# An attention pass with its steps in another order, 64x64 mask matmuls, and one block of cleared rows

## The chip, the core and the metric

The program runs on one core of a Trainium2 chip. Its engines run side by side, each through its own queue in order: TensorE (PE; PEld are its weight loads), VectorE (DVE), ScalarE (ACT), GpSimd (POOL) and SyncE (SP, which here only issues transfers). They wait for each other through semaphores. The metric is the device time of one execution in microseconds; lower is better.

## The reference

Attention for 8 x 8 heads of 576 positions and 64 dimensions, in two parts that are added: one over q, k and v averaged over four positions (144 positions, a full softmax), one over a local band. Then a layer of 8 experts for the 4608 rows of 512: each row goes to the one expert with the largest gate.

```
out_d = sm_attn(q_d, k_d, v_d)                  # mean over 4 positions
out_up = np.repeat(out_d, factor, axis=2)
mask = np.abs(pos[:, None] - pos[None, :]) < factor
scores = np.where(mask, scale * np.matmul(q, k.transpose(0, 1, 3, 2)), -1000000000.0)
out_local = np.matmul(softmax(scores), v)
x = (out_up + out_local) as rows of tokens
y[token] = gate[token] * (np.maximum(x @ w1[e], 0.0) @ w2[e])   # e = the token's expert
```

## The kernel before, in words

**Passes.** The attention runs in 32 passes, one for each pair of heads. The table `PASS` (L768) is the order of the steps inside a pass, written by hand. An entry `(step, lag)` does that step for pair `i - lag` while pass `i` runs, so up to five pairs are in work at once (lag -1 works ahead). As every engine takes its instructions in program order, this table alone sets the order on each engine. After the last pass three drain passes run, and then the stage of the experts.

Steps for the local band of pair i: `s_loc` (TensorE; mask matmuls L229, then 40 score matmuls L235, into pS, of which there is one), `max_loc` (VectorE L248), `sub_loc` (L252), `exp_loc` (ScalarE L255), `sums` (VectorE L258), `eps` (ScalarE L261), `inv` (VectorE L266, the reciprocal), `norm` (L270), `t_loc` (TensorE transposes L308 in two parts), `e_loc` (ScalarE copies them, L315), `pv_loc` (L336). For the averaged part: `pool_qk`, `pool_qk2`, `pool_v`, `pool_v2` on GpSimd; `s_d` (TensorE L284, into pD, of which there is one), `max_d` (L289), `max_scale` (L292), `exp_d` (ScalarE L298), `norm_d` (VectorE L273), `t_d` (L321), `e_d` (L329), `pv_d` (L349), `out_d` (ScalarE L353). `add_up` (VectorE L363) joins the two. The reciprocal of pair i-1 is written into the bank pD of pair i, so `inv` stands behind `s_d` of the running pass; `s_d` in turn waits for `exp_d` of the pass before, which reads the one pD. In the built program `exp_d` also waits for `norm_d` of the same pass.

**The router.** Entries that begin with "@" are slots for work on finished rows: `@ra` (40 or 32 router matmuls L381), `@rb` (their transposes L392 and L394, VectorE L397 to L408, an exponential L401), `@rc` (ranks and places: VectorE L423 to L436, ScalarE L426 and L428), `@x` (transposes L443 to rows, copied at L445), `@sc` (scatters of 128 rows to the table `xs`, a memset and an indirect transfer on GpSimd, L467 and L468), and `@w1` (a quarter of expert weights split on ScalarE L180 and GpSimd L181, passes 15 to 30). a, b and c of one group of rows fall into passes i, i+1 and i+2, a new group every four passes from pass 6; scatters run from pass 9. Transposes and router share three banks called pX.

**Loads.** At the start of pass i SyncE is given qk(i+2), vd(i+1) and vw(i), and in a few passes 512 KB of expert weights (raw). Three buffers each for qk and vw, two for vd, decide when a load can go.

**Cleared rows.** The table `xs` has for each expert a region with room; the rows behind the last token must read as padding. Its first 128 rows belong to no expert. At pass 20 SyncE writes the padding block `pad` (128 rows of 514, in SBUF) to them (L815) and to a table of its own, `zs` (L816). In the stage of the experts `pad_after` (L458) copies from `zs` behind an expert's rows. A write to `xs` is ordered behind the scatters that are out.

Of the kernel before, what the change touches and what calls it, by code (L numbers as in the profile page):

```python
# [90 lines left out]
def attention_moe_kernel(ctx: ExitStack, tc: tile.TileContext, qk, vw, vd, wg, w1, w2, cst, csb, out):  # L91
# [18 lines left out]
        return psX.tile([128, 512], F32, name="pX", bufs=3)  # L110

    xs = dram.tile([ROW0 + E * CAP, ROW], F32, name="xs")
    zs = dram.tile([128, ROW], F32, name="zs")

    QK, VW, VD, QKD, VDS, A, AD, AT, XT, MXD, SMD, ADT, PS_, PD, PV, IV, QKT, VDT, MX, BX = ({} for _ in range(20))

# [107 lines left out]
    def s_loc(i):  # L224
        p = psS.tile([128, 1024], F32, name="pS")
        PS_[i] = p
        for s in range(2):
            r = slice(s * 64, s * 64 + 64)
            nc.tensor.matmul(p[:, s * 512:s * 512 + NC * KW], selb[r], maskb[r], start=True, stop=False,  # L229
                             tile_position=(s * 64, 0), skip_group_check=True)  # L230
        x = QK[i]
        for c in range(NC):
            for h, t in ((0, 0), (1, 1), (0, 1), (1, 0)):
                g, s, r = NC * t + c, h ^ t, slice(h * 64, h * 64 + 64)
                nc.tensor.matmul(p[t * 64:t * 64 + QB, s * 512 + c * KW:s * 512 + (c + 1) * KW],  # L235
                                 x[r, g * QB:(g + 1) * QB],
                                 x[r, QPAD + g * QB:QPAD + g * QB + KW],
                                 start=False, stop=(c == NC - 1), skip_group_check=True)
# [219 lines left out]
    def pad_after(e):  # L458
        rs = nc.s_assert_within(rows_end(e), ROW0 + e * CAP, ROW0 + e * CAP + N, skip_runtime_bounds_check_because=why)
        nc.sync.dma_start(xs[bass.ds(rs, BASE), DM:].rearrange("(t p) c -> p t c", p=128),  # L460
                          zs[:, None, DM:].to_broadcast([128, BASE // 128, ROW - DM]))
        nc.sync.dma_start(xs[bass.ds(rs, 256), :DM].rearrange("(t p) c -> p t c", p=128),
                          zs[:, None, :DM].to_broadcast([128, 2, DM]))

    def scatter(m, t):
        xr = xrs[:, x_slot(m, t)]
# [297 lines left out]
    def at(k, fn, *a):  # L764
        todo.setdefault(k, []).append(lambda: fn(*a))


    PASS = (  # L768
        (s_loc, 0), (max_loc, 0), (pv_loc, 3), (pv_d, 3), (out_d, 3), (t_d, 2, 0), (e_d, 2, 0), (t_loc, 2, 1),
        (pool_qk, -1), (sums, 1), (s_d, 0), (eps, 1), (sub_loc, 0), (add_up, 3), (inv, 1), ("@rb",),  # L770
        (e_loc, 2, 1), (t_d, 2, 1), (t_loc, 2, 0), ("@sc",), (exp_loc, 0), (pool_qk2, -1), (max_d, 0),
        (e_d, 2, 1), (norm, 1), (e_loc, 2, 0), ("@rc",), (norm_d, 1), (pool_v, 0), ("@w1",), (max_scale, 0),
        ("@x",), (exp_d, 0), (pool_v2, 0), ("@ra",),
    )

    def steps(i):
# [29 lines left out]
    for i in range(NP):  # L806
        for fn, have, want in ((load_qk, QK, i + 2), (load_vd, VD, i + 1), (load_vw, VW, i)):
            for j in range(len(have), min(want, NP - 1) + 1):
                fn(j)
        if i == 2:  # L810
            nc.gpsimd.tensor_copy(crun, cf[:, C_CAP:C_CAP + E])
        if i in PADS:
            pad_first(PADS.index(i))
        if i == 20:
            nc.sync.dma_start(xs[0:ROW0, :], pad)  # L815
            nc.sync.dma_start(zs, pad)  # L816
        steps(i)
        if i + 1 < len(WARM):
            warm(WARM[i + 1], i >= 3)
        if i in RAW:  # L820
            raw_ahead(RAW.index(i) + 1)
        if i == NP - 1:
            close_p1.close()
            close_s.close()
            _, mp[0] = pool(name="m1", bufs=1)
            _, mp["p1"] = pool(name="psM1", bufs=2, space=PSUM)
            x_load(0, 0)
            gi_load(0, 0, 2)
            raw_ahead(8)
# [136 lines left out]
```

## Time and profile before

| what | us |
|---|---|
| median of three runs (656.22 to 662.75) | 657.36 |
| the profiled execution's own time | 659.0 |
| its span, first to last instruction | 657.2 |
| start of the maximum of pass 8, 20, 21, 24, 31 | 45.63, 118.09, 123.97, 145.47, 187.23 |

The span is what the trace shows; the time of an execution lies a little around it. A pass is read here from one start of VectorE's maximum (L248) to the next. In the rows, an idle time in brackets stands before the instruction, with what ended it ("issue": nothing that the profile shows).

### The profile page before, as it was taken

Reading aid. Unit: us, or ns where it says so; the run is one execution under the profiler, and the core shown is the slowest. Engines: PE = TensorE matmul, PEld = TensorE weight load, DVE = VectorE, ACT = ScalarE, POOL = GpSimd, SP = SyncE. Lnnn points to the kernel's source line nnn. Section 1 sums busy time; section 2 is a strip of 40 time slices with the busy share of each in tenths; the row PEclk is TensorE's granted clock in tenths of the full one; section 3 lists DMA queues with packets and bytes.
Section 4 is the critical chain, followed back from the end, with each engine's and each line's share of the span. In section 5 each row is a group of like instructions: output and inputs, shape, how many; then the busy total and the mean of one; then the engine's idle time right before and its main releaser. Section 6 shows DMA issues by size and latency. Waiting matters only on the chain.

```text
span 657.2 us, 15596 instructions
## 1 busy us (share of the span) xinstructions
PE 624.1 (95%) x6160; PEld 508.1 (77%) x6163; DVE 363.3 (55%) x674; ACT 321.3 (49%) x845; POOL 224.2 (34%) x333
## 2 busy tenths in 40 slices
PE   7999999899998989999999999999999999999994
PEld 4777777677777888888888888888888778888873
DVE  6999988878984565481481174175138047115020
ACT  3777777868874544452452263264235145224120
POOL 7968778798872410111111101111010101110111
PEclk9999999989998999999999999999999989999998
DMA  8999887987753496274284258248137528110001
GB/s 289 298 238 298 258 291 234 280 278 252 261 151 130 151 299 193 89 178 146 75 215 146 65 151 219 66 136 210 64 112 178 180 76 220 38 46 1 33 18 41
DMA packets 66226, 108.52 MB, mean 165 GB/s; under 512 B 15388, under 2 KB 36524, under 8 KB 66112
## 3 DMA queue, kind: packets, MB, share of 16 engines
q1 hardware_dynamic: 59984, 87.89, 46.8%
q0 software_dynamic: 5984, 19.01, 7.8%
q8 instruction: 66, 1.08, 0.7%
q14 instruction: 48, 0.39, 0.2%
q10 hardware_dynamic: 144, 0.15, 0.1%
HBM read 86.98 MB, written 23.67 MB: 168 GB/s over the span
## 4 chain that ended last, share of the span: by engine, by line
PE 72%; issue 10%; DVE 7%; DMA 3%; POOL 3%; ACT 3%; POOLq 0%; another core or an unknown queue 0%; SPq 0%; ACTq 0%; DVEq 0%
PE p L592 8%; PE p L593 8%; PE p L594 8%; PE p L606 7%; PE p L608 7%; PE p L607 7%; PE pD L284 3%; PE pS L235 2%; PE pX L308 2%; PE pX L321 2%; PE pX L443 2%; PE pX L688 2%; PE pX L707 2%; PE pPV L349 2%; PE pPV L336 1%
## 5 line engine op out<-in xcount | busy, mean ns | idle before, releaser
L592 PE MATMUL p<-xh,w1h 128*128 128x512 f32 (+1 forms) x288 | 107.3, 372 | 3.8 <-issue 1.8
L613 POOL DMA_INDIRECT out_dram<-y,tix x39 | 37.9, 973 | 210.4 <-ACT y L625 199.0
L593 PE MATMUL p<-xl,w1h 128*128 128x512 f32 (+1 forms) x288 | 106.4, 369 | 0.7 <-DVE xl L540 0.7
L594 PE MATMUL p<-xh,w1l 128*128 128x512 f32 (+1 forms) x288 | 106.2, 369 | 0.0
L606 PE MATMUL p<-w2h,hh 128*128 128x512 f32 x256 | 101.1, 395 | 0.0
L608 PE MATMUL p<-w2h,hl 128*128 128x512 f32 x256 | 99.8, 390 | 0.0
L607 PE MATMUL p<-w2l,hh 128*128 128x512 f32 x256 | 99.8, 390 | 0.0
L597 DVE SCALAR_TENSOR_TENSOR hl<-p,hh 128x512 fp32r<-128x512 f32 (+1 forms) x72 | 45.5, 632 | 96.6 <-ACT hh L596 96.4
L596 ACT ACTIVATE hh<-p 128x512 fp32r<-128x512 f32 (+1 forms) x72 | 39.8, 553 | 81.9 <-PE p L594 80.4
L625 ACT ACTIVATE y<-p,gi 128x512 f32<-128x512 f32 x32 | 22.1, 691 | 92.6 <-PE p L608 88.2
L592 PEld LDWEIGHTS p<-xh,w1h 128*128 128x128 f32 x288 | 55.1, 191 | 13.8 <-issue 2.2
L593 PEld LDWEIGHTS p<-xl,w1h 128*128 128x128 f32 x288 | 55.2, 192 | 9.8 <-DVE xl L540 0.9
L594 PEld LDWEIGHTS p<-xh,w1l 128*128 128x128 f32 x288 | 55.1, 191 | 9.0
L608 PEld LDWEIGHTS p<-w2h,hl 128*128 128x128 f32 x256 | 48.0, 188 | 10.3
L607 PEld LDWEIGHTS p<-w2l,hh 128*128 128x128 f32 x256 | 48.1, 188 | 10.1 <-DVE w2l L582 0.6
L606 PEld LDWEIGHTS p<-w2h,hh 128*128 128x128 f32 x256 | 48.1, 188 | 9.4
L468 POOL DMA_INDIRECT xs<-xr,ix x36 | 36.0, 1001 | 24.6 <-ACT re L401 10.9
L540 DVE TENSOR_TENSOR xl<-pX,xh 128x512 fp32r<-128x512 f32 x38 | 24.7, 684 | 35.2 <-ACT xh L539 34.2
L582 DVE TENSOR_TENSOR w2l<-raw,w2h 128x512 fp32r<-128x512 f32 x64 | 43.5, 682 | 0.8 <-ACT w2h L581 0.6
L298 ACT ACTIVATE AD<-pD,mxd 128x144 f32<-128x144 f32 x96 | 35.6, 380 | 13.6 <-DVE AD L273 10.9
L180 ACT ACTIVATE w1h<-raw 128x512 fp32r<-128x512 f32 (+1 forms) x72 | 41.6, 578 | 0.0
L215 POOL TENSOR_TENSOR vdt<-vd 72x512 f32<-72x512 f32 x32 | 40.8, 1275 | 0.1
(149 smaller groups left out, 1220.3 us busy)
## 6 DMA issues: line engine op xcount, KB each, us to landing
raw<-in_w_dram SPq DMA_DIRECT2D x64, 512.0 KB
qk<-in_qk_dram SPq DMA_DIRECT2D x32, 583.0 KB
vw<-in_vw_dram SPq DMA_DIRECT2D x32, 320.0 KB
vd<-in_vd_dram SPq DMA_DIRECT2D x32, 288.0 KB
xrow<-xs SPq DMA_DIRECT2D x32, 192.0 KB
xrow<-xs SPq DMA_DIRECT2D x32, 128.0 KB
xs<-zs SPq DMA_DIRECT2D x6, 512.0 KB
xs<-pad SPq DMA_DIRECT2D x3, 257.0 KB
```

The lines of the kernel that those rows point to most:

```text
L180: nc.scalar.activation(hi[:, s], src[:, s], AF.Copy)
L215: nc.gpsimd.tensor_add(t2, v[:, 0:2], v[:, 2:4])
L582: nc.vector.tensor_sub(lo, src, hi)
L592: nc.tensor.matmul(p, wh[:, fs], xh[:, k, r], start=(k == 0), stop=False)
L593: nc.tensor.matmul(p, wh[:, fs], xl[:, k, r], start=False, stop=False)
L594: nc.tensor.matmul(p, wl[:, fs], xh[:, k, r], start=False, stop=(k == 3))
L596: nc.scalar.activation(hh[:, f, r], p, AF.Relu)
L597: nc.vector.scalar_tensor_tensor(hl[:, f, r], p, 0.0, hh[:, f, r], op0=OP.max, op1=OP.subtract)
L606: nc.tensor.matmul(p, hh, wh, start=(f == 0), stop=False)
L607: nc.tensor.matmul(p, hh, wl, start=False, stop=False)
L608: nc.tensor.matmul(p, hl, wh, start=False, stop=(f == 7))
L613: ins = nc.gpsimd.indirect_dma_start(out=out, out_offset=bass.IndirectOffsetOnAxis(ap=ix, axis=0), in_=y, in_offset=None, bounds_check=N - ...
```

## The change

The order in `PASS` is another one (lags and slots are the same). The mask is added by four matmuls on 64x64 tiles in place of two on 64x128. `zs` is gone: `pad_after` copies from the first 128 rows of `xs`, and these are written in pass 8.

```diff
--- before.py
+++ after.py
@@ -110,7 +110,6 @@
         return psX.tile([128, 512], F32, name="pX", bufs=3)
 
     xs = dram.tile([ROW0 + E * CAP, ROW], F32, name="xs")
-    zs = dram.tile([128, ROW], F32, name="zs")
 
     QK, VW, VD, QKD, VDS, A, AD, AT, XT, MXD, SMD, ADT, PS_, PD, PV, IV, QKT, VDT, MX, BX = ({} for _ in range(20))
 
@@ -224,13 +223,14 @@
     def s_loc(i):
         p = psS.tile([128, 1024], F32, name="pS")
         PS_[i] = p
-        for s in range(2):
-            r = slice(s * 64, s * 64 + 64)
-            nc.tensor.matmul(p[:, s * 512:s * 512 + NC * KW], selb[r], maskb[r], start=True, stop=False,
-                             tile_position=(s * 64, 0), skip_group_check=True)
+        quads = ((0, 0), (1, 1), (0, 1), (1, 0))
+        for h, t in quads:
+            s, r, o = h ^ t, slice(h * 64, h * 64 + 64), slice(t * 64, t * 64 + 64)
+            nc.tensor.matmul(p[o, s * 512:s * 512 + NC * KW], selb[r, o], maskb[r], start=True, stop=False,
+                             skip_group_check=True)
         x = QK[i]
         for c in range(NC):
-            for h, t in ((0, 0), (1, 1), (0, 1), (1, 0)):
+            for h, t in quads:
                 g, s, r = NC * t + c, h ^ t, slice(h * 64, h * 64 + 64)
                 nc.tensor.matmul(p[t * 64:t * 64 + QB, s * 512 + c * KW:s * 512 + (c + 1) * KW],
                                  x[r, g * QB:(g + 1) * QB],
@@ -458,9 +458,9 @@
     def pad_after(e):
         rs = nc.s_assert_within(rows_end(e), ROW0 + e * CAP, ROW0 + e * CAP + N, skip_runtime_bounds_check_because=why)
         nc.sync.dma_start(xs[bass.ds(rs, BASE), DM:].rearrange("(t p) c -> p t c", p=128),
-                          zs[:, None, DM:].to_broadcast([128, BASE // 128, ROW - DM]))
+                          xs[0:ROW0, None, DM:].to_broadcast([128, BASE // 128, ROW - DM]))
         nc.sync.dma_start(xs[bass.ds(rs, 256), :DM].rearrange("(t p) c -> p t c", p=128),
-                          zs[:, None, :DM].to_broadcast([128, 2, DM]))
+                          xs[0:ROW0, None, :DM].to_broadcast([128, 2, DM]))
 
     def scatter(m, t):
         xr = xrs[:, x_slot(m, t)]
@@ -766,11 +766,11 @@
 
 
     PASS = (
-        (s_loc, 0), (max_loc, 0), (pv_loc, 3), (pv_d, 3), (out_d, 3), (t_d, 2, 0), (e_d, 2, 0), (t_loc, 2, 1),
-        (pool_qk, -1), (sums, 1), (s_d, 0), (eps, 1), (sub_loc, 0), (add_up, 3), (inv, 1), ("@rb",),
-        (e_loc, 2, 1), (t_d, 2, 1), (t_loc, 2, 0), ("@sc",), (exp_loc, 0), (pool_qk2, -1), (max_d, 0),
-        (e_d, 2, 1), (norm, 1), (e_loc, 2, 0), ("@rc",), (norm_d, 1), (pool_v, 0), ("@w1",), (max_scale, 0),
-        ("@x",), (exp_d, 0), (pool_v2, 0), ("@ra",),
+        (s_loc, 0), (sums, 1), (pool_qk, -1), (max_loc, 0), (pv_loc, 3), ("@rb",), (pv_d, 3), (t_loc, 2, 1),
+        (sub_loc, 0), (out_d, 3), (t_loc, 2, 0), (e_loc, 2, 1), (e_loc, 2, 0), (pool_qk2, -1), (t_d, 2, 0),
+        ("@sc",), (s_d, 0), (eps, 1), (e_d, 2, 0), (add_up, 3), (exp_loc, 0), (inv, 1), (pool_v, 0), ("@w1",),
+        (pool_v2, 0), (t_d, 2, 1), (max_d, 0), (norm, 1), ("@ra",), (e_d, 2, 1), ("@x",), (max_scale, 0),
+        (norm_d, 1), ("@rc",), (exp_d, 0),
     )
 
     def steps(i):
@@ -811,9 +811,8 @@
             nc.gpsimd.tensor_copy(crun, cf[:, C_CAP:C_CAP + E])
         if i in PADS:
             pad_first(PADS.index(i))
-        if i == 20:
+        if i == 8:
             nc.sync.dma_start(xs[0:ROW0, :], pad)
-            nc.sync.dma_start(zs, pad)
         steps(i)
         if i + 1 < len(WARM):
             warm(WARM[i + 1], i >= 3)
```

The changed file has one line less ahead of L113, so its line numbers there are smaller by one up to s_loc and after it again; names tell which is which.

VectorE in pass 27, in which the router's steps b fall (mx is the maximum, smd the sums, pD the reciprocal, rm to oh the router, A<-pS the subtraction, XT add_up). Before:

```order
L248 TENSOR_REDUCE mx<-pS 128x10
L258 TENSOR_REDUCE smd<-A 128x10
L252 TENSOR_TENSOR A<-pS,mx 128x2x5x64
L363 TENSOR_TENSOR XT<-pPV,outd_117 128x580
L266 RECIPROCAL pD<-smd 128x13
L397 TENSOR_REDUCE rm<-pX 128x5
L399 TENSOR_TENSOR pX<-pX,rm 128x40
L403 SCALAR_TENSOR_TENSOR pX<-pX,cf 128x40
L406 TENSOR_REDUCE rm<-pX 128x5
L408 TENSOR_TENSOR oh<-pX,rm 128x40
L289 TENSOR_REDUCE mxd<-pD 128x3
```

The same place in the changed kernel:

```order
L258 TENSOR_REDUCE smd<-A 128x10
L248 TENSOR_REDUCE mx<-pS 128x10
L397 TENSOR_REDUCE rm<-pX 128x5
L399 TENSOR_TENSOR pX<-pX,rm 128x40
L403 SCALAR_TENSOR_TENSOR pX<-pX,cf 128x40
L406 TENSOR_REDUCE rm<-pX 128x5
L408 TENSOR_TENSOR oh<-pX,rm 128x40
L252 TENSOR_TENSOR A<-pS,mx 128x2x5x64
L363 TENSOR_TENSOR XT<-pPV,outd_116 128x580
L266 RECIPROCAL pD<-smd 128x13
L289 TENSOR_REDUCE mxd<-pD 128x3
```

The sums now stand ahead of the maximum, and the router's five steps ahead of the subtraction and the reciprocal.

TensorE in the same pass, from the scores to the rows of tokens (pX<-cf,AD are t_d, pX<-cf,A t_loc, pD s_d, pX<-cf,lg the router's transposes). Before:

```order
L235 MATMUL pS<-qk 58x64 x20
L336 MATMUL pPV<-AT,vw 64x58 x20
L349 MATMUL pPV<-ADT,vds 64x144 x4
L321 MATMUL pX<-cf,AD 72x112 x3
L308 MATMUL pX<-cf,A 128x128 x2
L284 MATMUL pD<-qkd 64x144 x6
L392 MATMUL pX<-cf,lg 128x128
L394 MATMUL pX<-cf,lg 128x32
L321 MATMUL pX<-cf,AD 72x112 x3
L308 MATMUL pX<-cf,A 128x128 x3
L443 MATMUL pX<-cf,XT 128x128 x4
```

And in the changed kernel:

```order
L235 MATMUL pS<-qk 58x64 x20
L336 MATMUL pPV<-AT,vw 64x58 x20
L392 MATMUL pX<-cf,lg 128x128
L394 MATMUL pX<-cf,lg 128x32
L349 MATMUL pPV<-ADT,vds 64x144 x4
L308 MATMUL pX<-cf,A 128x128 x5
L321 MATMUL pX<-cf,AD 72x112 x3
L284 MATMUL pD<-qkd 64x144 x6
L321 MATMUL pX<-cf,AD 72x112 x3
L443 MATMUL pX<-cf,XT 128x128 x4
```

All five transposes of A stand ahead of s_d, and the router's transposes ahead of pv_d. (The list counts an fp32 matmul once; the trace shows two records for each.)

SyncE around pass 20, before:

```order
L119 DMA qk<-in_qk_dram 128x1166
L192 DMA vd<-in_vd_dram 72x1024
L196 DMA vw<-in_vw_dram 128x640
L815 DMA xs<-pad 128x514
L816 DMA zs<-pad 128x514
L119 DMA qk<-in_qk_dram 128x1166
```

And around pass 8 in the changed kernel:

```order
L118 DMA qk<-in_qk_dram 128x1166
L191 DMA vd<-in_vd_dram 72x1024
L195 DMA vw<-in_vw_dram 128x640
L815 DMA xs<-pad 128x514
L118 DMA qk<-in_qk_dram 128x1166
```

One write stands between the loads of pass 8 and pass 9 in place of two between those of pass 20 and 21.

## Rows read from the trace of the kernel before

**Rows 1.** Busy time by stretch; columns as the first line of the view names them.

```profile
core 0: us, PE busy (x) PEld busy (x) DVE busy (x) ACT busy (x) POOL busy (x), PEclk, DMA share, GB/s
45.63:123.97 78.34, 73.32 (x1708) 58.13 (x1705) 70.15 (x148) 60.12 (x216) 61.94 (x80) 1.00 0.86 270
123.97:145.47 21.50, 18.22 (x366) 14.16 (x367) 15.92 (x30) 14.51 (x52) 18.52 (x26) 0.92 0.93 285
145.47:187.23 41.76, 39.56 (x928) 31.73 (x923) 37.18 (x76) 34.85 (x126) 37.18 (x49) 1.00 0.73 238
45.63:69.15 23.52, 22.09 (x531) 17.60 (x530) 21.40 (x44) 17.82 (x64) 18.20 (x24) 1.00 0.91 291
...
151.30:175.35 24.05, 22.38 (x520) 17.82 (x522) 21.50 (x46) 19.13 (x69) 21.62 (x29) 1.00 0.77 252
```

**Rows 2.** VectorE in order of time: start, us, instruction, idle before and releaser.

```profile
62.73 0.82 DVE L248 TENSOR_REDUCE mx<-pS 128x10 f32<-128x640 f32 x1 [0.94 <-PE pS L235]
...
86.53 0.82 DVE L248 TENSOR_REDUCE mx<-pS 128x10 f32<-128x640 f32 x1 [1.15 <-PE pS L235]
...
105.57 0.82 DVE L248 TENSOR_REDUCE mx<-pS 128x10 f32<-128x640 f32 x1 [0.53 <-PE pS L235]
...
111.72 0.82 DVE L248 TENSOR_REDUCE mx<-pS 128x10 f32<-128x640 f32 x1 [1.16 <-PE pS L235]
...
156.82 0.82 DVE L248 TENSOR_REDUCE mx<-pS 128x10 f32<-128x640 f32 x1 [0.55 <-PE pS L235]
...
162.97 0.83 DVE L248 TENSOR_REDUCE mx<-pS 128x10 f32<-128x640 f32 x1 [1.16 <-PE pS L235]
...
180.87 0.82 DVE L248 TENSOR_REDUCE mx<-pS 128x10 f32<-128x640 f32 x1 [0.47 <-PE pS L235]
...
187.23 0.82 DVE L248 TENSOR_REDUCE mx<-pS 128x10 f32<-128x640 f32 x1 [1.38 <-PE pS L235]
```

**Rows 3.** VectorE in order of time, pass 26: after the sums, and the last step.

```profile
157.56 0.81 DVE L258 TENSOR_REDUCE smd<-A 128x10 f32<-128x640 f32 x1
158.29 0.81 DVE L252 TENSOR_TENSOR A<-pS,mx 128x640 f32<-128x640 f32 x1
...
161.21 0.60 DVE L273 TENSOR_TENSOR AD<-AD,pD 128x432 f32<-128x432 f32 x1
```

**Rows 4.** TensorE in order of time, end of pass 26 and start of pass 27.

```profile
159.78 0.49 PE L308 MATMUL pX<-cf,A 128*128 128x128 f32 x3
...
160.64 1.30 PE L381 MATMUL pX<-XT,wgt 128*32 128x128 f32 x40
161.87 0.31 PE L229 MATMUL pS<-cb 64*128 64x320 bf16 x2
162.11 0.79 PE L235 MATMUL pS<-qk 64*58 64x64 f32 x40
162.72 0.75 PE L336 MATMUL pPV<-AT,vw 64*64 64x58 f32 x40
```

**Rows 5.** SyncE and TensorE in order of time, passes 20 and 22.

```profile
118.67 0.33 SPq L196 DMA_DIRECT2D vw<-in_vw_dram  x1
121.76 0.34 SPq L815 DMA_DIRECT2D xs<-pad  x1
...
122.62 0.45 SPq L119 DMA_DIRECT2D qk<-in_qk_dram  x1
...
129.62 0.33 PE L235 MATMUL pS<-qk 64*58 64x64 f32 x8 [1.16 <-issue]
```

**Rows 6.** The page: its head and a row of its transfer issues.

```profile
span 657.2 us, 15596 instructions
...
zs<-pad SPq DMA_DIRECT2D x1, 257.0 KB
```

**Rows 7.** VectorE's waits, passes 8 to 31 (us, times, longest); TensorE in pass 27.

```profile
DVE pX L403 <- ACT re L401: 1.6, 5, 0.3
...
167.27 0.55 PE L308 MATMUL pX<-cf,A 128*128 128x128 f32 x3 [0.93 <-ACT re L401]
```

**Rows 8.** ScalarE in order of time, start of pass 27.

```profile
161.91 0.38 ACT L298 ACTIVATE AD<-pD,mxd 128x144 f32<-128x144 f32 x1 [0.24 <-DVE AD L273]
```

**Rows 9.** GpSimd's waits from 85.4 to 193.4 us (us, times, longest).

```profile
POOL w1l L181 <- ACT w1h L180: 9.3, 6, 2.7
```

## The prediction

> **What bounds the kernel now.** The stages first: the table of busy time by stretch [rows 1]. From the maximum of pass 8 (45.63 us) to that of pass 31 (187.23 us) lie 23 passes in 141.6 us. VectorE is busy there for 70.15 + 15.92 + 37.18 = 123.25 us, so 18.35 us are idle; TensorE is busy 131.1 us, GpSimd 117.6. Nothing has much room, but VectorE is the engine whose idle time can be read: its matter is to be late once per pass. The reader is to see three unlike stretches: 78.34 us for 13 passes (6.03 each), 21.50 us for only three (7.17 each), 41.76 us for seven (5.97). After the passes comes the stage of the experts, TensorE's own matmuls one behind the other; the change doesn't touch its order, so what the passes give back should reach the end.
>
> Then VectorE's own rows. Its maximum (L248) has to wait for the scores: eight waits outside the long stretch, 0.94, 1.15, 0.53, 1.16, 0.55, 1.16, 0.47 and 1.38 us [rows 2], 7.34 us in all. Between them nothing is idle: in pass 26 the sums start 0.74 us after the maximum, and the last multiplication ends at 161.81, 4.99 us after it [rows 2, 3].
>
> Why the scores are late is in TensorE's rows [rows 4]. Behind the second part of the transposes (L308) stand the tokens' rows and, one pass in four, the 40 router matmuls: 1.23 us from their start to the masks. Masks and scores follow, and VectorE's maximum begins 0.25 us after the next step (162.72) has begun on TensorE. So a pass with the router makes TensorE some 1.2 us longer than VectorE, and VectorE has nothing else in its queue ahead of the maximum. In the pass after, the router's VectorE steps make VectorE the longer one: work and waiting lie in the wrong passes.
>
> Last the long stretch. SyncE issues vw at 118.67 (0.33 us) and then stands until 121.76, when the write of cleared rows (L815) may go: it writes the table that the scatters write, and waits for the last of them. The next qk load leaves at 122.62 [rows 5]. The held loads and two writes of 257 KB [rows 6] leave together; in the stretch behind it the DMA share is 0.93, the highest shown in [rows 1]. In the middle of 40 score matmuls, where no semaphore is waited for, TensorE stands for 1.16 us (it resumes at 129.62) [rows 5], and the granted clock of the stretch is 0.92 against 1.00 before and behind it [rows 1]: part of it ran at the lower level, 1.2 GHz.
>
> **The change, part by part.**
> *The cleared rows.* In pass 8 no scatter is out yet (the first is in pass 9), so L815 has nothing to wait for and the loads behind it aren't held; the second block (zs), 257 KB, is gone, and the later pads read the rows of xs instead: same bytes, off TensorE's path. Three passes at the mean of the other twenty, (78.34 + 41.76) / 20 = 6.01 us, are 18.0; the stretch took 21.50: **-3.5 us**. Ends: 0 if the wait only coincided with the slow passes, -3.5 if it is the cause; I take the latter, because hole, clock and DMA share stand together right behind it. Against it: pass 8 gets 257 KB; at the 291 GB/s of passes 8 to 11 [rows 1] that is 0.9 us of transfers in front of loads that are needed about two passes later: I take a third, **+0.3**.
>
> *The sums first.* VectorE now does the sums of the pass before (0.73 us from start to start, 157.56 to 158.29 [rows 3]) ahead of the maximum. Their input was made a pass earlier, so they run while the scores are late. Each wait falls by the smaller of itself and 0.73: 0.73, 0.73, 0.53, 0.73, 0.55, 0.73, 0.47, 0.73, together **-5.2 us**. This holds only if nothing waits instead. Next in line is the reciprocal: it waits for the downsampled scores (L284), and TensorE now reaches them one group of transposes later, since all five L308 stand ahead of them; the 0.49 us recorded for the three moved ones [rows 4] would come back in any pass where TensorE is the late one. What covers it is the second move: the router's VectorE steps, which stood behind the reciprocal, now stand ahead of the subtraction, in just the pass that follows the long TensorE pass. Ends: 0 (all comes back at the reciprocal) to -16.7 (all idle time, less the 1.6 us in which the router's steps wait for ScalarE within themselves [rows 7]).
>
> *The router on the other engines.* Its transposes go ahead of pv_d on TensorE; before, the three L308 waited 0.93 us for a bank that ScalarE's exponential held back [rows 7], and ScalarE stood too. Now that exponential is ahead of the copies, and the banks are needed later. I count no gain: it is the same lateness that the first term already prices. Steps c go behind norm_d on VectorE and ahead of exp_d on ScalarE, two small instructions; exp_d starts as soon as norm_d is through (161.91 [rows 8]) and VectorE has steps c to do meanwhile: 0.
>
> *GpSimd.* pool_qk2 goes ahead of the scatters, so each scatter and its memset leave one such step later and the second halving a scatter earlier; the rows are read only after the passes: 0. The w1 piece goes ahead of steps c on ScalarE; GpSimd stood 9.3 us for it in six waits [rows 9]. That is room on an engine off the path, no term of its own. On SyncE only the write moves; qk, vd and vw keep their order.
>
> *The masks.* Four matmuls of 64x64 for two of 64x128, with 64 more weight loads and matmuls in all. Now 0.24 us pass from the first mask to the first score matmul [rows 4]. The nearest rows are those behind them: 40 score matmuls in the same four tiles and the same order go in 0.61 us, 15 ns each [rows 4], which they can only do side by side. So four masks should take what two took: 0. Ends per pass: -0.1 (part of the 0.24 is the change of tile) to +0.72 (four in a row at 0.24 each).
> The Trainium skill, "TensorEngine Tiling (Array Packing)", section Restrictions and Gotchas, speaks against it: matmuls of different row tiles can't use one PSUM bank at the same time. The first two masks have different row tiles and one bank. The scores have the same pairs, and their rows don't bear the rule out.
>
> **Sum.** 659.0 (the profiled execution; its span is 657.2 [rows 6]) - 3.5 + 0.3 - 5.2 = 650.6 us. The median of the three runs, 657.36, lies 1.64 us below the profiled one: **649.0 us**.
>
> **Rivals.**
> *The transfers or GpSimd take over.* At the forecast a pass takes 6.0 - 0.35 = 5.65 us, four of them 22.6. In passes 8 to 11 the DMA engines work 0.91 of 23.52 us = 21.4, so their share would be 0.95; GpSimd has 21.62 us of work in 24.05 where it also splits w1 [rows 1]. For it: both leave about 1 us in four passes. Against: VectorE waits for no load in these rows, and passes 8 to 11 ran at 0.91 without one. Then only the long stretch gives: 659.0 - 3.2 - 1.6 = 654.2. Chance 0.25.
> *More comes back.* The router's lateness goes with the sums' and VectorE runs near its floor: half of the way from 5.2 to 16.7, some 6 us more, 643. Chance 0.10. Against it: holes like that of [rows 5] have no cause in the order and stay.
> *The masks don't overlap*, the slower side. Place: between the last transposes and the scores, each pass. TensorE is busy 22.38 of 24.05 us [rows 1], 0.42 us free per pass; below that an addition mostly hides, above it TensorE sets the pass. One after the other: +0.72, of which 0.30 x 23 passes = 6.9 us show, and nothing of the sums' gain is left: 659.0 + 6.9 - 1.6 = 664.3, or 661.1 with the 3.2 us of the long stretch. Chance 0.06. In pairs, +0.24 a pass: at most 5.5 us, 654.5; chance 0.04. By the Trainium skill's rule on banks, named above, it would be the pairs.
>
> **Numbers.** Forecast, 649.0 with a range of its own of 646 to 652: 0.55. A measurement of this kernel tells about 1% (6.6 us) from no change, so faster means below 650.8: four fifths of the forecast, the 0.10 with more, a little of the rest: 0.58. Within 1%: the other fifth, nearly all of the first rival, the pairs: 0.36. Slower: 0.06. The range that leaves out 2 in 10 reaches from the better case, 643, over the first rival to 656.
>
> **What would show it.** Right: the maximum's waits for the scores sum to under 3 us between passes 8 and 31, with the sums in the row ahead; the reciprocal waits for L284 less than 1 us in all; SyncE's L815 follows vw without a gap; the three passes behind pass 20 take about 18 us at a granted clock of 1.00; four masks and then the first score after 0.24 us; the maximum of pass 31 near 179. Wrong: idle time ahead of the reciprocal that grows as that of the maximum falls; GpSimd or loads named as releasers of VectorE or TensorE; a hole in the scores at another pass with the clock at its lower level; score matmuls that start 0.4 us or more behind the masks; or passes that shrink and an expert stage that begins no earlier.

## The result, and the profile after

The changed kernel took 652.81 us (median of four runs, 651.46 to 663.92) against 656.79 us of before (four runs too): 0.9881 of it, with an interval of 0.9833 to 0.9929. Its profiled execution took 653.26 us, with a span of 651.5. Measured twice more, with 12 runs each time, it came out at 0.9974 (0.9934 to 1.0014) and 0.9969 (0.9933 to 1.0005): some 2 us, and both intervals still hold "no change". The forecast of 649.0 promised 8.4 us. The ratios leave disturbed runs out, so they differ a little from those of the medians.

Busy time by stage: from max_loc of pass 8 to that of pass 31, from there to the first L606, and from there to the end (columns as in [rows 1]). First the changed kernel, then a second profile of before:

```profile
46.15:186.12 139.97, 129.57 (x2990) 106.08 (x2992) 127.77 (x253) 105.85 (x386) 120.11 (x156) 0.98 0.84 262
186.12:221.13 35.01, 29.77 (x425) 25.93 (x417) 21.21 (x54) 20.71 (x63) 13.94 (x29) 1.00 0.45 139
221.13:651.48 430.35, 419.62 (x1923) 347.73 (x1921) 180.94 (x300) 163.36 (x298) 54.69 (x106) 0.99 0.44 125
```

```profile
45.74:181.97 136.23, 128.52 (x2987) 102.32 (x2984) 123.36 (x253) 108.62 (x393) 117.15 (x154) 1.00 0.89 274
181.97:216.59 34.62, 30.93 (x425) 27.16 (x417) 21.89 (x56) 20.36 (x59) 15.66 (x31) 0.95 0.43 141
216.59:652.85 436.26, 421.49 (x1923) 348.90 (x1921) 180.66 (x299) 163.39 (x297) 54.87 (x106) 0.99 0.45 123
```

The reader is to see three things. The passes of before took 136.2 us this time, not 141.6 as in [rows 1]: one kernel's passes differ by more than 5 us between two executions. VectorE's busy time doesn't: 123.25 and 123.36 us before, 127.77 after. And the experts, whose order nothing touched, are 5.9 us shorter here.

VectorE's waits in the passes of the changed kernel (us, times, longest):

```profile
DVE pD L266 <- PE pD L284: 3.5, 2, 2.1
DVE rm L397 <- PE pX L394: 1.6, 1, 1.6
DVE pX L403 <- ACT re L401: 1.0, 3, 0.3
DVE pD L266 <- PE pX L443: 0.8, 1, 0.8
DVE pD L266 <- ACT A L255: 0.8, 1, 0.8
```

The waits of max_loc for the scores are gone, but for one of 0.3 us (9.1 us in eight in the second profile of before). In their place stand waits ahead of the reciprocal and the router's maximum (the latter behind a hole of TensorE of 1.3 us in pass 27).

TensorE and SyncE in order of time: the masks of pass 28, and the cleared rows of pass 8.

```profile
166.56 0.33 PE L229 MATMUL pS<-cb 64*64 64x320 bf16 x4
166.72 0.73 PE L235 MATMUL pS<-qk 64*58 64x64 f32 x40
```

```profile
45.58 0.34 SPq L195 DMA_DIRECT2D vw<-in_vw_dram  x1
45.97 0.82 SPq L815 DMA_DIRECT2D xs<-pad  x1
46.84 0.42 SPq L118 DMA_DIRECT2D qk<-in_qk_dram  x1
```

Four masks need 0.16 us up to the first score, two needed 0.24 [rows 4]; the median of the passes is the same. The four start within 0.01 us of each other. SyncE doesn't stand any more.

Where the busy time of VectorE grew: steps c of pass 24, and GpSimd at the same time.

```profile
147.95 0.17 DVE L425 TENSOR_REDUCE gt<-re 128x4 f32<-128x32 f32 x1
148.05 0.18 DVE L430 TENSOR_TENSOR rk<-pX,oh 128x32 f32<-128x32 f32 x1
148.14 0.89 DVE L431 TENSOR_TENSOR crun<-crun,cs 128x8 f32<-128x8 f32 x1
148.95 0.17 DVE L433 TENSOR_REDUCE pos<-rk 128x4 f32<-128x32 f32 x1
149.16 0.61 DVE L435 CAST ix<-pos 128x4 int32<-128x4 f32 x1
149.69 0.17 DVE L436 RECIPROCAL xr<-gt 128x4 f32<-128x4 f32 x1
```

```profile
147.85 1.16 POOL L203 TENSOR_TENSOR qkt<-qk 128x576 f32<-128x576 f32 x1
149.08 0.67 POOL L209 TENSOR_TENSOR qkd<-qkt 128x288 f32<-128x288 f32 x1
```

An addition of 8 elements takes 0.89 us and ends as GpSimd's halving ends; the cast behind it ends with the next halving. In the first profile of before the same two took 0.16 and 0.17 us, and GpSimd was standing for w1l at that time (1.50 us, up to 150.88).

```profile
150.17 0.16 DVE L431 TENSOR_TENSOR crun<-crun,cs 128x8 f32<-128x8 f32 x1
150.51 0.17 DVE L435 CAST ix<-pos 128x4 int32<-128x4 f32 x1
150.88 0.73 POOL L181 TENSOR_TENSOR w1l<-raw,w1h 128x256 fp32r<-128x256 f32 x1 [1.50 <-ACT w1h L180]
```

The second profile of before shows that the order alone is not the reason: in its pass 24 GpSimd did not stand, and there, in the old order, the two took 0.79 and 0.56 us.

### The profile page after: what moved, and what is told of

Read it like the earlier page. It is cut to its first block, busy times and chain, and to the rows that moved or that the text cites. A ratio compares the mean times of both kernels' runs of the same rounds, so it can differ in the third digit from the quotient of the medians.

```text
span 651.5 us, 15716 instructions
## 1 busy us (share of the span) xinstructions
PE 619.4 (95%) x6224; PEld 509.2 (78%) x6227; DVE 368.7 (57%) x674; ACT 318.4 (49%) x845; POOL 225.1 (35%) x333
## 4 chain that ended last, share of the span: by engine, by line
PE 70%; issue 11%; DVE 9%; POOL 3%; DMA 3%; ACT 3%; POOLq 0%; another core or an unknown queue 0%; SPq 0%; DVEq 0%; ACTq 0%
PE p L593 8%; PE p L592 8%; PE p L594 8%; PE p L606 7%; PE p L608 7%; PE p L607 7%; PE pD L284 3%; PE pX L321 2%; PE pX L688 2%; PE pX L707 2%; PE pS L235 2%; PE pPV L336 1%; PE pPV L349 1%; PE pX L308 1%; DVE A L270 1%
## 5 line engine op out<-in xcount | busy, mean ns | idle before, releaser
L592 PE MATMUL p<-xh,w1h 128*128 128x512 f32 (+1 forms) x288 | 105.9, 368 | 1.1 <-DVE hl L597 0.8
L606 PE MATMUL p<-w2h,hh 128*128 128x512 f32 x256 | 101.2, 395 | 0.0
L606 PEld LDWEIGHTS p<-w2h,hh 128*128 128x128 f32 x256 | 48.1, 188 | 9.4
```

The lines of the kernel that those rows point to most:

```text
L592: nc.tensor.matmul(p, wh[:, fs], xh[:, k, r], start=(k == 0), stop=False)
L606: nc.tensor.matmul(p, hh, wh, start=(f == 0), stop=False)
```

## The experiments

All in one table: passes (max_loc of pass 8 to 31), middle, experts (first L606 to the end) of each profile in us, the median of the runs, and the ratio to before on the same chip with its interval. Before had a median of 660.33 beside changed again, order alone, counts in PSUM and max first, 657.28 beside masks alone, rows alone, code shift and sums alone, and 657.25 beside the last four. Order alone and code shift have 6 runs, max first 11, the others behind the first comparison 12.

```
kernel                  passes  middle  experts  median  ratio
before, first profile   141.60  35.07   434.88
changed, first profile  139.97  35.01   430.35   652.81  0.9881 (0.9833-0.9929)
changed again           140.73  35.66   431.13   657.39  0.9974 (0.9934-1.0014)
order alone             136.31  34.23   436.88   655.38  0.9871 (0.9814-0.9928)
counts in PSUM          135.92  34.91   430.89   654.02  0.9881 (0.9843-0.9919)
max first               141.61  34.43   430.05   654.95  0.9923 (0.9889-0.9957)
masks alone             139.85  35.26   430.56   657.70  1.0024 (0.9996-1.0052)
rows alone              134.19  37.03   437.16   657.52  1.0022 (0.9985-1.0059)
code shift              146.96  36.73   434.51   668.86  1.0213 (1.0161-1.0264)
sums alone              135.46  35.37   436.88   657.78  1.0009 (0.9973-1.0046)
before again            136.23  34.62   436.26   656.05  0.9994 (0.9961-1.0027)
counts again            134.60  36.17   430.86   652.19  0.9938 (0.9902-0.9974)
order and counts        134.89  36.06   433.45   654.40  0.9955 (0.9917-0.9993)
changed, third          137.22  37.61   430.19   654.71  0.9969 (0.9933-1.0005)
```

**The size of the gain**: the changed kernel again (no edit).

> The changed kernel once more, unaltered, for the size of the gain. In the pair of profiles the attention passes end only 1.1 us earlier (max_loc of pass 31 at 186.12 us against 187.23), while the stage of the experts is 4.1 us shorter (427.2 us against 431.3); of these 4.1, the profile of before has one TensorE hole of 1.8 us and a stretch at half clock at 528 us, and another half-clock stretch at 200 us. Theory A: those are accidents of one execution, the gain of the medians is 3 to 4.5 us (ratio 0.993 to 0.995), and a new profile shows the experts at any length between 427 and 431 us. Theory B: the new order makes the experts themselves shorter; then the stage is 427 us again and the ratio is near 0.991.

The gain is smaller than theory A had it, but the experts took 431.1 us again (the 427 us of the expectation count from a later start), as theory B had it. That called for the next three.

**The order alone.**

```diff
-        (s_loc, 0), (max_loc, 0), (pv_loc, 3), (pv_d, 3), (out_d, 3), (t_d, 2, 0), (e_d, 2, 0), (t_loc, 2, 1),
...
+        (s_loc, 0), (sums, 1), (pool_qk, -1), (max_loc, 0), (pv_loc, 3), ("@rb",), (pv_d, 3), (t_loc, 2, 1),
...
```

> Before with the new order of steps alone: two mask matmuls of 128 rows, the cleared rows and their second block at pass 20 as before. Theory A: the order carries the whole gain; the masks and the cleared rows are worth under 0.5 us each, so the time equals that of the changed kernel within 1 us, and max_loc waits for the scores hardly at all (under 1 us between passes 8 and 31, against 10.9). Theory B (the term on record for the cleared rows): the stand of SyncE at pass 20 costs 3.5 us, so this kernel is 3 to 4 us slower than the changed one. Whichever holds, the steps of the router behind norm_d should take 1.9 us in place of 0.95, since the order of GpSimd is the same as in the changed kernel.

```profile
46.55:182.86 136.31, 129.19 (x2947) 103.33 (x2945) 128.60 (x254) 105.81 (x386) 119.60 (x155) 1.00 0.88 271
```

max_loc's waits for the scores, here and then in the second profile of before:

```profile
DVE mx L248 <- PE pS L235: 1.7, 2, 1.3
```

```profile
DVE mx L248 <- PE pS L235: 9.1, 8, 1.6
```

Beside the second profile of before, with the same masks and rows, this is the cleanest pair. max_loc waits 7.4 us less, and VectorE's idle time falls from 136.23 - 123.36 = 12.87 us to 136.31 - 128.60 = 7.71: 2.2 us of other idle time have come. Its busy time grows by 5.24, and the passes are as long as they were. The time of six runs is nevertheless below that of before, and below the changed kernel's on that chip. I read nothing from it: the first four runs of the changed kernel gave a ratio as low, and longer series did not bear it out. The 3 to 4 us of theory B aren't there, and theory A's match within 1 us isn't either. The additions and casts (busy us and mean ns between the bars), here and in the second profile of before:

```profile
L431 DVE TENSOR_TENSOR crun<-crun,cs 128x8 f32<-128x8 f32 x6 | 3.5, 583 | 0.0
L435 DVE CAST ix<-pos 128x4 int32<-128x4 f32 (+1 forms) x6 | 3.1, 524 | 0.2
```

```profile
L431 DVE TENSOR_TENSOR crun<-crun,cs 128x8 f32<-128x8 f32 x6 | 1.6, 267 | 0.0
L435 DVE CAST ix<-pos 128x4 int32<-128x4 f32 (+1 forms) x6 | 1.4, 236 | 0.2
```

That is (583 - 267 + 524 - 236) ns x 6 = 3.6 of the 5.24 us. Most of the rest lies with sub_loc, which in the passes without the router's steps b now stands right behind max_loc and waits for its result. In the changed kernel:

```profile
143.54 0.81 DVE L248 TENSOR_REDUCE mx<-pS 128x10 f32<-128x640 f32 x1
144.39 0.82 DVE L252 TENSOR_TENSOR A<-pS,mx 128x640 f32<-128x640 f32 x1
```

It starts 0.85 us behind it, where independent steps start 0.74 us apart [rows 2, 3]. In five of the 23 passes the router's steps stand between the two, so it is 0.11 us in 18 passes: 2.0 us, 0.6 of them idle and the others busy.

**The two small tiles in PSUM.**

```diff
-        cs = rp.tile([128, E], F32, name="cs")
+        cs = p[:, 64:64 + E]
-        pos = rp.tile([128, 5], F32, name="pos")
+        pos = p[:, 80:85]
```

> The changed kernel with two small tiles of the router (the count cs and the position pos) put into the PSUM bank that the step already holds; no instruction is moved. In the changed kernel the addition of the counts takes 515 ns on average (160 before) and the cast of the positions 316 to 466 ns (172 before); each ends where a GpSimd instruction ends (148.95 us and 149.69 us in pass 25). Theory A: a VectorE operation that has all its operands in SBUF stands until GpSimd's running operation on SBUF is done. With one operand in PSUM it does not; then the addition is back near 0.2 us and the cast near 0.2 us in all passes, VectorE is 3.4 us less busy over the passes, and the time falls by 2 to 3.5 us (to 0.995 to 0.997 of the changed kernel). Theory B: the two operations wait for something that belongs to their place behind norm_d (a tensor that is late, the row of instructions); then they stay at 0.4 to 0.5 us and the time does not move. Theory C: they get short, but the passes are held by loads or TensorE, and the time does not move.

The addition and the cast are back at 0.15 and 0.16 us, as theory A has it. Run a second time:

> The changed kernel with cs and pos in PSUM, once more, unaltered, beside the changed kernel on the same chip. Theory A (VectorE stands at GpSimd's operations only where all operands lie in SBUF): 2 to 5 us faster than the changed kernel again (the first time the means were 652.4 and 657.0 us), additions of the counts and casts under 0.2 us. Rival: the first difference was the luck of that chip; then the two are within 1.5 us.

Steps c of the second run's pass 24, and GpSimd at the same time:

```profile
145.13 0.15 DVE L431 TENSOR_TENSOR crun<-crun,pX 128x8 f32<-128x8 f32 x1
145.32 0.20 DVE L433 TENSOR_REDUCE pX<-rk 128x4 f32<-128x32 f32 x1
145.55 0.16 DVE L435 CAST ix<-pX 128x4 int32<-128x4 f32 x1
```

```profile
144.80 1.14 POOL L203 TENSOR_TENSOR qkt<-qk 128x576 f32<-128x576 f32 x1
```

The same halving runs, and neither operation waits for it. VectorE's busy time in the passes is 125.32 and 125.04 us, against 127.77, 128.86 and 128.70 in the changed kernel's three profiles. The medians lie 3.4 us (654.02 for 657.39) and 2.5 us (652.19 for 654.71) below the changed kernel's on the same chips, and both ratios to before are below 1 with their intervals: on both chips the fastest version of those run eleven times or more. The Trainium skill, "SBUF — State Buffer", section "SBUF: two separate sides", says that VectorE and GpSimd share a pair of ports, that one instruction holds it to its end, and that a VectorE operation with two inputs in SBUF meets there a GpSimd operation that reads SBUF, as does one in a two-port mode. The rows agree for the addition (two inputs in SBUF). The cast has one, so by that rule it must run in such a mode, which no row shows. The reductions beside them have one input in SBUF and don't wait (0.17 us for L425 at 147.95 us, during the same halving). As L425 goes from SBUF to SBUF, theory A's wording, "all its operands in SBUF", is too wide.

**max_loc first again.**

```diff
-        (s_loc, 0), (sums, 1), (pool_qk, -1), (max_loc, 0), ...
+        (s_loc, 0), (pool_qk, -1), (max_loc, 0), (sums, 1), ...
```

> The changed kernel with the sums of the pass before behind max_loc again, between it and sub_loc; all else as in the changed kernel. Theory A (the term on record: the sums cover the end of the scores): max_loc waits for the scores again, some 8 to 11 us over the passes, while each pass wins back 0.11 us because an independent step stands again between max_loc and sub_loc (23 passes, 2.5 us); in sum 3 to 6 us slower than the changed kernel. Theory B: in the new order the scores are early anyway, because t_d and e_d that stood ahead of them were moved; then the waits stay under 2 us and the kernel is 1 to 2.5 us faster than the changed one.

max_loc's waits come back, 6.0 us in seven:

```profile
DVE mx L248 <- PE pS L235: 6.0, 7, 1.3
```

Yet the kernel isn't slower than the changed one (0.9923 against 0.9974, the intervals overlap). So theory A is right in that waits come back, if fewer than its 8 to 11 us, and its price of 3 to 6 us is out; theory B has the waits wrong, and whether its gain is there stays open. In this order no gain from the place of the sums can be seen: what they cover, the dependent pair behind them and other waits may well cost.

**The sums alone**, in the order of before.

```diff
-        (s_loc, 0), (max_loc, 0), ... (pool_qk, -1), (sums, 1), (s_d, 0), ...
+        (s_loc, 0), (sums, 1), (max_loc, 0), ... (pool_qk, -1), (s_d, 0), ...
```

> Before with one step moved: the sums of the pass before stand ahead of max_loc in place of behind the scores' followers; all else as before. The term on record is 5.2 us faster. Theory A: the sums cover the end of the scores, but max_loc and sub_loc now stand next to each other and cost 0.11 us more per pass (2.5 us over 23 passes); so the waits of max_loc for L235 fall from 10.9 us to under 2, and the passes 8 to 31 get 3 to 6 us shorter (136 to 139 us in place of 141.6); the stand at 525 us stays, since TensorE's program is unaltered. Theory B: TensorE (0.92 busy in the passes) is the bound behind the waits; then the waits turn up ahead of the reciprocal or the sum of outputs, and the passes stay within 1.5 us of 141.6.

```profile
DVE pD L266 <- PE pD L284: 2.5, 7, 0.4
DVE mx L248 <- PE pS L235: 2.0, 5, 0.6
```

max_loc waits 7.1 us less than in the second profile of before, but the reciprocal 2.3 us more (0.2 there), and VectorE is busy 126.04 us in place of 123.36. The passes are 0.8 us shorter than in that profile and the time is that of before (1.0009): theory B's outcome. That TensorE is the bound is not shown by it, as 2.7 us of the price are busy time of VectorE.

**The cleared rows alone.**

```diff
-        if i == 20:
+        if i == 8:
             nc.sync.dma_start(xs[0:ROW0, :], pad)
-            nc.sync.dma_start(zs, pad)
...
-                          zs[:, None, DM:].to_broadcast([128, BASE // 128, ROW - DM]))
+                          xs[0:ROW0, None, DM:].to_broadcast([128, BASE // 128, ROW - DM]))
```

> Before with the cleared rows alone: one block, written in pass 8, and no zs; order and masks as before. The term on record is 3.5 us faster, because TensorE's hole at 129.6 us and its half-clock stretch go with SyncE's stand at pass 20. Theory A: the instruction fetch makes that hole and the one in the experts, and the cleared rows move no instruction of TensorE; then holes of over 0.6 us stay in the passes, the stand at 525 us stays too (from the first L606 to the end 434 to 437 us), and the time is that of before within 1.5 us. Theory B: SyncE's stand made the hole of pass 22; then max_loc of pass 24 comes 3 us sooner (142.5 us) and stays so. Theory C: zs made the stand in the experts; then their stage is 430 to 431.5 us.

No gain in time (the interval leaves room for 1 us), and the experts keep their stand, so zs doesn't make it: theory A for the whole, but not for the holes of over 0.6 us in the passes; the longest without a releaser is 0.5 us here. The passes are 2.0 us shorter than in the second profile of before, the middle 2.4 us longer, at a clock of 0.86. What the second profile of before shows at pass 20 decides more:

```profile
116.10 0.46 SPq L196 DMA_DIRECT2D vw<-in_vw_dram  x1
118.50 0.34 SPq L815 DMA_DIRECT2D xs<-pad  x1
```

```profile
118.20:136.00 17.80, 17.06 (x397) 13.75 (x395) 16.05 (x35) 13.89 (x53) 15.49 (x21) 1.00 0.94 279
```

SyncE stands there as in [rows 5] (1.9 us, 2.8 in the first profile), and in the 17.8 us behind it nothing happens: clock 1.00, DMA share 0.94. The next hole, 1.27 us in the scores of pass 24, ends at 139.39 us, and no half clock follows it. The changed kernel, whose SyncE doesn't stand, has a hole of 0.8 to 1.4 us between 117 and 128 us in each of its three profiles. So the hole and the half clock of the first profile were that execution's and not the stand's. The three passes behind pass 20 are 1.3 us longer in the second profile than three at the mean of its other twenty; the sum had 3.5.

**The masks alone**, and **only the position of TensorE's instructions**.

```diff
-        for s in range(2):
-            r = slice(s * 64, s * 64 + 64)
...
+        quads = ((0, 0), (1, 1), (0, 1), (1, 0))
+        for h, t in quads:
+            s, r, o = h ^ t, slice(h * 64, h * 64 + 64), slice(t * 64, t * 64 + 64)
...
```

> Before with the four 64x64 mask matmuls alone; order of steps and cleared rows as before. TensorE's program gets 128 instructions longer ahead of the experts (two matmuls and two weight loads in each of 32 passes). So far the two kernels with two mask matmuls (before and the one with the new order alone) show a stand of TensorE of 1.8 and 2.35 us ahead of L592 at 525 and 521 us, behind a branch and with an instruction fetch under way, and a stretch of 3.4 us at half clock behind it; the four profiles with four mask matmuls show neither. Theory A: where the blocks of the instruction fetch lie against the branches decides that stand, so it is gone here: from the first L606 to the end 430 to 431.5 us (before: 434.9), the passes as before (max_loc from pass 8 to 31: 141.6 us), the time 3 to 4 us shorter. Theory B: the stand belongs to the second block of cleared rows (zs); then it is still here, the stage is 434 to 437 us and the time that of before within 1 us.

```diff
-    warm(WARM[0])
+    warm(WARM[0] - 4)
+    for _ in range(64):
+        nc.tensor.matmul(wp[:, :16], wsrc[:, :128], wsrc[:, :16], start=True, stop=True)
```

> Before with nothing changed but the warm-up at the start: 4 of its first 9 matmuls of 512 columns give way to 64 matmuls of 16 columns, which makes TensorE's program 120 instructions longer ahead of everything else, about as much as the four masks do, and does no other work. Theory A (position of the instruction blocks): the stand ahead of L592 at 525 us and the half clock behind it are gone, from the first L606 to the end 430 to 431.5 us, and holes in the passes lie at other places than in before. Theory B (the masks themselves or zs): the stage stays 434 to 437 us with its stand. The start may move by 1 us either way, so the stage is the gauge and not the whole time.

TensorE in order of time in the experts, in the second profile of before; the branch ahead of it (min, median, max ns of two); and the stretches before, in and behind the hole:

```profile
519.99 0.39 PE L594 MATMUL p<-xh,w1l 128*128 128x512 f32 x1
522.74 0.50 PE L592 MATMUL p<-xh,w1h 128*128 128x512 f32 x1 [2.36 <-issue]
```

```profile
L742 PEldq COMPARE_BRANCH  x2: 82/1982/3881, 510.0 to 515.5; - x2
```

```profile
516.70:520.30 3.60, 3.60 (x17) 2.63 (x15) 0.00 (x0) 0.44 (x1) 0.00 (x0) 1.00 0.23 79
520.40:522.70 2.30, 0.00 (x0) 0.00 (x0) 0.00 (x0) 0.15 (x1) 0.97 (x1) 1.00 0.13 51
524.10:527.50 3.40, 3.40 (x10) 2.61 (x9) 1.01 (x2) 1.63 (x3) 0.00 (x0) 0.50 0.00 0
```

The branch of 3.9 us at 515.5 is covered by work already queued. From it on the instruction queue fetches one block after the other (transfers of 16 KB start at 516.64, 520.10 and 523.89 us), and TensorE runs dry for 2.36 us; 1.4 us after it resumes, the clock drops to half for 3.4 us. The stand is there, between 519 and 528 us, in all six profiles with two masks and the old warm-up (before twice, order, sums, rows, order and counts), and in none of the seven with four masks. Masks alone takes it away (430.56 us). The branch is as long there (3.82 us at 517.8), but only two transfers belong to it (518.79 and 522.27); the next starts 11.8 us later, where in all six profiles with the stand it starts 3.3 to 4.0 us later. With the warm-up alone lengthened it is gone from there too, but another has appeared behind another branch:

```profile
330.06 0.50 PE L596 MATMUL p<-xh,w1l 128*128 128x512 f32 x1 [2.02 <-issue]
```

Theory A is right that position decides (neither the masks nor zs were touched), and wrong that the experts would then be 430 to 431.5 us: 434.5. In the passes the same shift does worse, with stands of 2.0, 1.7, 1.3, 1.2 and 1.1 us and a clock of 0.95; it makes the kernel 2.1% slower, with 1 us of that in the start (max_loc of pass 8 at 46.75 us for 45.74). The masks may pay in the passes as well (139.85 us, among others a stand of 2.1 us at 109.6), which would be why masks alone is not faster than before and misses the 3 to 4 us of its theory A. Such holes too go with the transfers of instructions: in the passes of all 14 profiles TensorE has 30 holes of over 0.7 us without a releaser, and each begins 0.2 to 2.0 us behind the start of a transfer of 16 KB. There are 332 such transfers, so most make no hole. And their places follow the program: all six profiles with the new order and four masks have a hole of 1.0 to 2.1 us at pv_loc of pass 27, and no profile with two masks has one there. The Trainium skill, "Runtime: NRT & Kernel Launch", section "Instruction fetch mechanics", says that instructions come in blocks of 16 KB and that a taken branch out of the fetched window stalls the engine until the block is there. The branch of 3.9 us with its transfer agrees. By the same section, going from block to block in straight code is mostly hidden; the passes have no branch of TensorE, and their 30 holes, up to 2.1 us each, are what was not hidden.

**Before again.** (No edit.)

> The kernel before once more, unaltered, for a second profile and for what two sets of runs of one kernel differ by. From max_loc of pass 8 to that of pass 31 the profile of before took 141.6 us, those of before with the sums moved and of before with the cleared rows alone 135.5 and 134.2 us, and yet neither of these two is faster in its timed runs (1.001 and 1.002 of before). Theory A: the passes of one and the same kernel differ by some 6 us from execution to execution, with the holes of the instruction fetch and the half clock behind them, and the first profile of before was one of the long ones; then this profile has 134 to 139 us there. Theory B: the passes of before always take 140 to 143 us, and the two edits lose elsewhere what they gain there. Under both the stand of about 2 us ahead of L592 in the experts, at 520 to 527 us, is there again, and the stage from the first L606 to the end takes 434 to 438 us. The ratio should be 0.997 to 1.003.

Theory A: 136.2 us for the passes, 0.9994 for the ratio, the stand at 520 us.

**The order with the two tiles in PSUM**, masks and rows as before.

> Before with the new order of steps and with cs and pos in PSUM; two mask matmuls of 128 rows, zs and the cleared rows at pass 20 as before. It asks what the masks and the rows are worth in the better version. Theory A: the masks count only by where they put the instruction blocks; then the stand at about 518 us and half clock behind it are back (from the first L606 to the end 434 to 438 us in place of 430.9), the passes take 134 to 138 us, and the kernel is 2 to 5 us slower than the one with masks and rows as changed. Theory B: the stand costs nothing in the whole, because the kernels without it lose as much in the passes; then the two are within 1.5 us.

```profile
216.93:650.38 433.45, 419.50 (x1923) 347.89 (x1921) 180.66 (x299) 163.25 (x297) 55.62 (x106) 1.00 0.45 124
```

The stand came back (2.2 us at 519 us), the half clock behind it didn't: 2.6 us longer than with four masks. The medians differ by 2.2 us (654.40 and 652.19), the intervals overlap: as theory A has it, but not shown. Asked a third time, the changed kernel gave the ratio told at the head, which is theory A's least gain, with theory B inside the interval:

> The changed kernel a third time, unaltered, for the size of its gain: the first comparison gave 0.988 (0.983 to 0.993) of before, the second 0.997 (0.993 to 1.001). Theory A: the gain is 2 to 5 us (0.992 to 0.997), made of a stand in the experts that the masks move away (4 to 6 us in profiles), waits of VectorE that go, and small operations that get longer. Theory B: there is no gain to be measured (0.998 to 1.002).

## Why the prediction held, and where its steps failed

The range held the first result, and the direction was right. That is luck more than mechanism: rows alone and sums alone, the two large terms by themselves, took the time of before, and what the profiles gain lies in the experts, for which the sum had nothing. The forecast itself, 8.4 us and most of the chance on more than 1%, was not right: the two longer comparisons say 0.3%, which is the case "within 1%". By its own steps:

*The cleared rows, -3.5 us: failed.* "Hole, clock and DMA share stand together right behind it" was a coincidence. In the second profile of before SyncE stands just the same, and for 17.8 us neither a hole nor a lower clock follows. The step took a stretch of one execution for the kernel's; the lower end, 0, was right to within the 1 us that rows alone can tell. The +0.3 us for the write in pass 8 is too small for any run here to show.

*The sums first, -5.2 us: the waits went, the time didn't.* In order alone max_loc waits 7.4 us less, other idle time is 2.2 us more, and the difference is the 5.2 us of the sum by chance: its eight waits were those of another execution. What failed is "this holds only if nothing waits instead": I looked for waits, and the price came as busy time, 5.24 us.

*Steps c behind norm_d, 0: failed.* This is 3.6 of those 5.24 us. [rows 9] showed GpSimd standing 9.3 us in six waits, and I called it room on an engine off the path. It was the gap in which steps c ran undisturbed. In the new order the w1 piece stands ahead of steps c, so the wait is over before they start (at 146.47 us in pass 24, where they start at 147.84), and GpSimd's halvings run beside them.

*The dependent pair.* That sub_loc now follows directly on max_loc was in the order and not in the sum: 0.11 us in each of 18 passes, 2.0 us.

*The masks, 0: right for what they take.* 0.16 us for four, and the Trainium skill's rule on banks ("TensorEngine Tiling (Array Packing)", Restrictions and Gotchas), by which they would go in pairs, isn't borne out here, where the two masks that share a bank write different halves of its partitions. But the sum held nothing for 128 more instructions ahead of the rest of TensorE's program: 5.7 us less in the experts and 3.6 more in the passes (masks alone beside the second profile of before; the latter is within what the passes of one kernel differ by).

*"What the passes give back should reach the end": wrong place.* The passes gave back nothing that can be told from their spread (141.6 and 136.2 us before; 140.0, 140.7 and 137.2 after); the experts gave some 5 us (434.9 and 436.3 before; 430.4, 431.1 and 430.2 after).

Of the signs that were named: max_loc's waits under 3 us, L815 behind vw and the masks came true. The reciprocal's waits for L284 were 3.5, 3.5 and 1.7 us, not under 1; the three passes behind pass 20 took 20.5 us at first and 18.5 and 18.4 later, against 21.5 and 18.9 before; the maximum of pass 31 stood at 186 us, not at 179. Of the first rival, the transfers had no share in it: in the three profiles of the changed kernel neither VectorE nor TensorE waits for a load. GpSimd had a share, not as an engine that others wait for but as one beside which VectorE's operations get longer. Holes at other passes with the clock at half level behind them, a sign of the wrong case, came at 117 us (1.4 us) and 135 us (1.3 us).

What stays open is what the gain of some 2 us is made of. If the experts give 5 us, the stages ahead of them take some 3 back, and that is less than the passes of one kernel differ by from one execution to the next. Nor is it settled what masks and rows are worth beside the order: on one chip the changed kernel was slower than order alone (657.39 and 655.38 us), on another, with the two tiles in PSUM, the version with them was faster (652.19 and 654.40).

## What to carry to other kernels

An idle engine off the path can be what keeps a resource free: before closing its gap, look at which operations of a neighbour run inside it, and whether both work in SBUF. When a wait is covered by moving work into it, sum busy and idle time of the waiting engine both, since the moved steps may leave a dependent pair without a buffer between them. And before a stretch of a few us is priced as a cause, take a second profile of the same kernel; here VectorE's busy time repeated to 1%, while the same stretch of the same kernel differed by 4%.

## What the runs showed that I had not expected

- A VectorE operation of 4 to 8 elements per partition took up to 1.01 us beside a GpSimd halving of 1.15 us (an addition in max first), and 0.15 to 0.17 us beside the same halving once one operand lay in PSUM.
- 120 more TensorE instructions at the very start, with almost no work, made the kernel 2.1% slower (668.86 against 657.28 us). Behind the warm-up only the place against the instruction blocks is another, and its profile has five holes in the passes, 7.4 us in all, each behind a transfer of instructions.
- A TensorE hole of about 2 us is often followed by a stretch at half clock. Of the 14 holes of 1.7 to 2.4 us in all profiles 11 had one of 3.4 us within 2.5 us of their end, which costs another 1.7 us (an estimate: half of the stretch). Behind the other three, one of them the stand at 519 us of order and counts, none came.
